# A linear-attention and Swish layer on one core: the order of work under the first output phase rearranged

## Chip, cores and metric

The kernel runs on one core of one Trainium2 chip. The metric is the device time of an execution in microseconds (us). TensorE's granted clock was 1.00 in the profile before. Times are medians of 3 to 12 runs. A ratio is the mean time of one kernel's fast runs over that of the other's fast runs of the same rounds, so it isn't quite the ratio of the medians quoted beside it.

## The reference

Linear attention with phi(x) = elu(x) + 1, then a two-layer product with Swish between, over 8 batches of 576 tokens, 8 heads of 64, and 2048 hidden features.

```python
def _attn_ref(q, k, v):                     # [8, 8, 576, 64] each
    phi = lambda x: np.where(x > 0, x, np.exp(x) - 1.0) + 1.0
    q_p, k_p = phi(q), phi(k)
    kv  = np.einsum('bhsd,bhse->bhde', k_p, v)
    num = np.einsum('bhsd,bhde->bhse', q_p, kv)
    den = np.einsum('bhsd,bhd->bhs', q_p, np.sum(k_p, axis=2))[..., None] + 1e-06
    return num / den
# x = attention output as [4608, 512]
h = x @ w_in                                # [512, 2048]
g = h * (1.0 / (1.0 + np.exp(-beta * h)))
out = g @ w_out                             # [2048, 512]
```

## The kernel before

The program is one hand-ordered stream per engine. For each batch b there are two phases on TensorE: Hb (x @ w_in, followed by Silu on ScalarE) and Yb (g @ w_out). The attention of batch b+1 is slipped in between the matmuls of both by a plan: a table from a step to functions that run after that step. Silu is called with scale beta, so w_out is divided by beta once, in four quarters (`w_out_scale`), as soon as each has landed. w_out lands in fp32 in buffers that later hold other things.

Two PSUM (matmul output memory) pairs of banks serve attention (`attps`, tag "att"), four single banks the large products. The last four groups of H0 borrow both pairs.

```python
    def w_out_scale(i, dve=True):
        for c in range(4):
            ...                                   # dst, src, by = rbeta[:, ff]
            if dve:
                nc.vector.tensor_scalar(dst, src, by, None, ALU.mult)
            else:
                nc.scalar.activation(dst, src, ACTF.Copy, scale=by)

    def h_last(b, x, between):
        hps = []
        for i in range(2):
            hp = att_banks()
            for ii in range(2):
                h_mm(b, x, hp[:, ii], 12 + 2 * i + ii, 0, 4)
                hps.append(hp[:, ii])
        for f in between:
            f()
        for i in range(4):
            silu(b, 12 + i, hps[i])

    def y_phase_wide(b, plan):                    # four tiles side by side, ff outermost
        yp = [mm_bank([P, DM]) for _ in range(4)]
        for ff in range(12):
            for t in range(4):
                y_mm(b, yp[t], t, ff)
            run(plan, ff)
        for t in range(4):
            for ff in range(12, FC):
                y_mm(b, yp[t], t, ff)
            y_out(b, t, yp[t], on_act=True)
            run(plan, 12 + t)

    # loads on GpSimd's queue, in this order: ... w_out 0, w_out 1, k 1, q 1, then
    load_w_out(2)
    load_v(1)
    load_w_out(3)
    # H0's plan (cut)
            17: [F(w_out_scale, 0)],
            19: [F(begin, 1), F(relu, 1, 1), F(relu, 1, 0)],
    # then
    clear_tail(2)
    load_next(2)
    h_last(0, xT[0], [F(exp_, 1, 1), F(exp_, 1, 0), F(w_out_scale, 2, dve=False)])
    w_out_scale(1)
    y_phase_wide(0, {
        4: [F(phi, 1, 1), F(v_copy, 1), F(phi, 1, 0), F(load_next, 3)],
        8: [F(kv_mm, 1), F(kv_evac, 1)],
        9: [F(q_trans, 1, 0, 1, wide=True), F(q_trans, 1, 2, 3, wide=True),
            F(w_out_scale, 3)],
        ...
    })
```

An index such as `relu, 1, 1` means batch 1, operand 1 (k); operand 0 is q. "KV" below is the product of phi(k) and v (`kv_mm`); its copy out of PSUM is `kv_evac`.

## Time and profile before

| | before |
|---|---|
| device time, median of 3 | 299.17 us (298.81 to 299.87) |
| profiled span | 297.2 us |
| TensorE busy | 284.8 us, 96% |
| ScalarE, VectorE busy | 177.2 and 125.0 us |
| Y0 on TensorE, from its first matmul to H1's first | 34.12 to 54.91 us |
| the same work by the spacing of matmuls | 17.63 us |

In the rows of a timeline the columns are: start, length from the first start to the last end, engine, source line, operation, output and inputs, and a count; in brackets stands the idle time of the engine before the row and what ended it. A row without brackets followed the one before it with hardly any idle time (the shortest that was printed is 0.16 us). L500 is a matmul of Y, L448 of H, L339 KV, L375 the transposes of phi(q), L394 the num products, L428 the transposes of x. On the other engines, L228 is an exp, L440 a Silu, L211 and L213 the scaling of w_out, L236 a relu, L241 phi, L350 the copy of KV, L410 the last step of a normalisation. A few matmul records are missing from each trace, so that a count of 3 or 15 can stand for 4 or 16. The rows themselves are in the prediction.

### The profile page before, as it was taken

What the parts mean: (1) busy time and instruction counts of PE and PEld (TensorE: products, weight loads), DVE (VectorE), ACT (ScalarE), POOL (GpSimd) and SP (SyncE); (2) the same over time, 40 slices, a digit from 0 to 9 for tenths busy, and PEclk for the clock granted to TensorE, in tenths of its full rate; (3) what the DMA queues carried; (4) which work ended last, traced back from release to release, by engine and by line L of the source; (5) the groups of instructions that cost most, each with busy time, mean ns of one, the idle gap of its engine ahead of it and who ended that gap; (6) DMA issues with size and microseconds to landing.
All of it is one profiled execution on the core that took longest, in us unless ns stands there. A gap on an engine that the chain in (4) does not pass through costs nothing.

```text
span 297.2 us, 4721 instructions
## 1 busy us (share of the span) xinstructions
PE 284.8 (96%) x1876; PEld 144.6 (49%) x1897; DVE 125.0 (42%) x263; ACT 177.2 (60%) x235; POOL 52.1 (18%) x72
## 2 busy tenths in 40 slices
PE   8789978999999999999999999999999999999994
PEld 3466435744556454445444544454445444444443
DVE  5774298504574154715471547154715400110012
ACT  2788795879988790779076907690660068008500
POOL 8925465723004100140011000000000000000000
PEclk9999999999999999999999999999999999999999
DMA  7999999999928954599457255024502400020032
GB/s 110 192 207 342 258 270 191 240 208 187 149 89 170 185 95 117 124 154 160 115 124 82 71 117 124 1 73 115 120 5 72 117 36 0 35 84 25 0 72 72
DMA packets 69206, 36.43 MB, mean 123 GB/s; under 512 B 37808, under 2 KB 63680, under 8 KB 69184
## 3 DMA queue, kind: packets, MB, share of 16 engines
q0 software_dynamic: 38400, 20.45, 47.4%
q1 hardware_dynamic: 30624, 15.55, 20.0%
q8 instruction: 15, 0.25, 0.3%
q10 hardware_dynamic: 160, 0.13, 0.2%
q14 instruction: 7, 0.06, 0.1%
HBM read 36.71 MB, written 9.44 MB: 155 GB/s over the span
## 4 chain that ended last, share of the span: by engine, by line
PE 71%; DMA 17%; ACT 6%; POOL 3%; issue 2%; DVE 0%; POOLq 0%; ACTq 0%
PE mm L448 33%; PE mm L500 32%; DMA xqk<-in_q_dram 5%; DMA xqk<-in_k_dram 4%; DMA vraw<-in_v_dram 4%; DMA w_in<-in_moe_w_in_dram 4%; PE att L394 2%; ACT e L228 2%; PE att L339 2%; POOL xqk L132 1%; PE mm L532 1%; ACT g L440 1%; ACT L228 1%; ACT w_out L213 1%; POOL vraw L132 1%
## 5 line engine op out<-in xcount | busy, mean ns | idle before, releaser
L440 ACT ACTIVATE g<-mm,beta_c 128x512 bf16<-128x512 f32 (+2 forms) x156 | 97.4, 632 | 88.4 <-PE mm L448 87.9
L500 PE MATMUL mm<-w_out,g 128*128 128x512 bf16 x541 | 127.5, 379 | 2.5 <-DVE w_out L211 1.3
L448 PE MATMUL mm<-xT,w_in 128*128 128x512 bf16 (+2 forms) x560 | 107.8, 349 | 1.0 <-DVE xT L365 0.5
L448 PEld LDWEIGHTS <-w_in 128*128 128x128 bf16 x656 | 62.2, 98 | 61.9 <-issue 0.9
L500 PEld LDWEIGHTS <-g 128*128 128x128 bf16 x560 | 52.8, 98 | 58.5 <-issue 1.6
L510 DVE COPY y_sb<-mm 128x512 f32<-128x512 f32 x27 | 18.7, 691 | 70.4 <-PE mm L500 68.2
L228 ACT ACTIVATE e<-xqk 128x2560 bf16<-128x2560 bf16 x14 | 31.9, 2329 | 0.1
L410 DVE TENSOR_TENSOR xs<-att,rden 128x512 bf16<-128x512 f32 (+1 forms) x40 | 27.6, 689 | 1.6 <-DVE rden L409 0.2
L241 DVE TENSOR_TENSOR qk_p<-r,e 128x2560 bf16<-128x2560 bf16 x14 | 20.9, 1490 | 14.6 <-ACT e L228 13.9
L350 DVE CAST kv_bd<-att 64x130 bf16<-64x130 f32 x28 | 8.2, 292 | 35.0 <-PE att L339 34.7
L72 POOL DMA_DIRECT2D vraw<-in_v_dram x7 | 6.2, 881 | 78.3 <-DVE vaug L365 70.9
L408 DVE TENSOR_SCALAR den<-att 128x8 f32<-128x8 f32 (+1 forms) x40 | 6.5, 161 | 27.1 <-PE att L394 27.0
L394 PEld LDWEIGHTS <-q_pT 128*128 128x128 bf16 (+1 forms) x160 | 11.7, 100 | 10.9 <-issue 2.7
L394 PE MATMUL att<-kv_bd,q_pT 128*128 128x130 bf16 (+1 forms) x160 | 15.8, 221 | 1.1 <-ACT q_pT L367 0.4
L236 DVE TENSOR_SCALAR r<-xqk 128x2560 bf16<-128x2560 bf16 x14 | 11.9, 858 | 7.2 <-DMA xqk<-in_k_dram 4.9
L448 PE MATMUL mm<-xT_tail,w_in 128*128 128x512 bf16 x63 | 13.9, 379 | 0.1
L567 PE MATMUL mm<-g 128*128 128x512 bf16 x35 | 10.0, 440 | 1.2 <-DVE g L144 1.2
L228 ACT ACT_TABLE_LOAD x7 | 9.0, 1283 | 1.6 <-DMA xqk<-in_k_dram 1.5
L409 DVE RECIPROCAL rden<-den 128x8 f32<-128x8 f32 (+1 forms) x40 | 8.1, 202 | 1.4
L72 POOL DMA_DIRECT2D xqk<-in_k_dram x7 | 6.2, 891 | 12.8 <-ACT e L228 6.5
L76 POOL DMA_DIRECT2D xqk<-in_k_dram x7 | 7.6, 1082 | 2.7 <-DMA w_in<-in_moe_w_in_dram 2.7
L440 ACT ACT_TABLE_LOAD x6 | 7.7, 1283 | 0.1
(73 smaller groups left out, 140.5 us busy)
## 6 DMA issues: line engine op xcount, KB each, us to landing
out_dram<-y_sb SPq DMA_DIRECT2D x28, 256.0 KB, 2.3
xqk<-in_k_dram POOLq DMA_DIRECT2D x7, 512.0 KB, 10.7
xqk<-in_q_dram POOLq DMA_DIRECT2D x7, 512.0 KB, 12.0
vraw<-in_v_dram POOLq DMA_DIRECT2D x7, 512.0 KB, 11.5
w_in<-in_moe_w_in_dram POOLq DMA_DIRECT2D x4, 512.0 KB, 11.5
g<-in_moe_w_out_dram POOLq DMA_DIRECT2D x4, 512.0 KB, 11.0
out_dram<-y_sb SPq DMA_DIRECT2D x14, 128.0 KB, 5.1
xqk<-in_moe_w_out_dram POOLq DMA_DIRECT2D x2, 512.0 KB, 14.8
```

The lines of the kernel that those rows point to most:

```text
L72: eng.dma_start(out=dst[:, :, 0:NJ, :].rearrange("p h j d -> p h (j d)"), in_=src[b, :, 0:MAIN, :].rearrange("h (p j) d -> p h (j d)", j=NJ),)
L228: nc.scalar.activation(st[b, "e", a][:, h0:h1], xqk[b % NX][:, a, h0:h1], ACTF.Exp)
L236: nc.vector.tensor_scalar(st[b, "r", a][:, h0:h1], xqk[b % NX][:, a, h0:h1], 0.0, 1.0, ALU.max, ALU.add)
L241: nc.vector.tensor_tensor(st[b, "p"][:, a].rearrange("p j (h d) -> p h j d", h=H)[:, h0:h1], st[b, "r", a][:, h0:h1], st[b, "e", a][:, h0: ...
L350: nc.vector.tensor_copy(kv_bd[b % 2][i][gs, :, g, :], st[b, "kvp"][gs, 2 * i : 2 * i + 2, :])
L394: nc.tensor.matmul(nps[:n, p // 2, c0 : c0 + 2 * (D + 1)], st[b, "qT"][:, t, p, :n], kv_bd[b % 2][p // 2][:, p % 2], start=True, stop=True ...
L410: nc.vector.tensor_mul(xs[:n], nv[:, :, :, 0:D], rden[:n, :, :, None].to_broadcast([n, 2, 4, D]))
L440: nc.scalar.activation(g_sb[b % 2][:, ff, c0:c1], hp[:, c0:c1], ACTF.Silu, scale=beta_c[:, ff : ff + 1],)
L448: nc.tensor.matmul(hp[:, c0:c1], w_in_sb[ff // 4][:, kc, (ff % 4) * P : (ff % 4 + 1) * P], x[:, t0:t1, kc, :] if b < B else x[:, kc, c0:c1 ...
L500: nc.tensor.matmul(yp, g_sb[b % 2][:, ff, t * P : (t + 1) * P], w_out_sb[ff // 4][:, ff % 4, :], start=(ff == 0), stop=(ff == FC - 1),)
L510: nc.vector.tensor_copy(y_sb, yp)
L567: nc.tensor.matmul(st["warm"], g_sb[0][:, FC - 1, 0:P], g_sb[0][:, FC - 1, :], start=True, stop=True, skip_group_check=True,)
```

## The change

Its intent is to take three waits of TensorE out of Y0: that for the second quarter of w_out, that of KV for the Silus, and that of the first num product.

```diff
     h_phase(0, ...,
-            3: [F(x_trans, 0, 1), F(num_mm, 0, 2), F(num_norm, 0, 2)],
+            3: [F(x_trans, 0, 1, dve=True), F(num_mm, 0, 2), F(num_norm, 0, 2),
+                lambda: q_out0(3, st["qb2"], 256, False)],     # was on VectorE, earlier
...
-            17: [F(w_out_scale, 0)],
-            19: [F(begin, 1), F(relu, 1, 1), F(relu, 1, 0)],
+            17: [F(w_out_scale, 0), F(w_out_scale, 1)],
     clear_tail(2)
     load_next(2)
-    h_last(0, xT[0], [F(exp_, 1, 1), F(exp_, 1, 0), F(w_out_scale, 2, dve=False)])
-    w_out_scale(1)
+    h_last(0, xT[0], [])
+    begin(1)
+    exp_(1, 1)
+    exp_(1, 0)
+    silu_table()
+    relu(1, 1)
+    relu(1, 0)
+    w_out_scale(2)
+    phi(1, 1)
+    v_copy(1)
+    phi(1, 0)
     y_phase_wide(0, {
-        4: [F(phi, 1, 1), F(v_copy, 1), F(phi, 1, 0), F(load_next, 3)],
-        8: [F(kv_mm, 1), F(kv_evac, 1)],
-        9: [F(q_trans, 1, 0, 1, wide=True), F(q_trans, 1, 2, 3, wide=True),
-            F(w_out_scale, 3)],
-        10: [F(q_trans, 1, 4, wide=True), F(num_mm, 1, 0), F(num_norm, 1, 0)],
-        11: [F(num_mm, 1, 1), F(num_norm, 1, 1)],
-        12: [F(num_mm, 1, 2), F(num_norm, 1, 2), F(x_trans, 1, 0, wide=True)],
-        13: [F(num_mm, 1, 3), F(num_norm, 1, 3), F(x_trans, 1, 1, wide=True)],
-        14: [F(num_mm, 1, 4), F(num_norm, 1, 4), F(x_trans, 1, 2, wide=True)],
+        4: [F(load_next, 3)],
+        9: [F(kv_mm, 1), F(kv_evac, 1), F(w_out_scale, 3)],
+        10: [F(q_trans, 1, 0, 1, wide=True), F(q_trans, 1, 2, 3, wide=True)],
+        11: [F(num_mm, 1, 0), F(num_norm, 1, 0)],
+        12: [F(num_mm, 1, 1), F(num_norm, 1, 1), F(x_trans, 1, 0, wide=True)],
+        13: [F(num_mm, 1, 2), F(num_norm, 1, 2), F(x_trans, 1, 1, wide=True)],
+        14: [F(num_mm, 1, 3), F(num_norm, 1, 3), F(q_trans, 1, 4, wide=True)],
     })
     h_phase(1, ..., {
+            0: [F(x_trans, 1, 2), F(num_mm, 1, 4), F(num_norm, 1, 4)],
             1: [F(x_trans, 1, 3)],
```

On VectorE `clear_tail(2)`, a memset of 0.48 us, stood behind the relus and now stands ahead of them, since the relus moved.

More of the change, by code (lines that the diff above doesn't have):

```diff
@@ L641, in q_second @@
         q_out0(2, qb2, 0, False)
-        q_out0(3, qb2, 256, True)
+        st["qb2"] = qb2
     h_phase(
```

## The prediction

> **What bounds the kernel now.** I read the page first, then the table of stretches, then the timelines of TensorE, ScalarE and VectorE from 30 to 56 us, then the waits of that stretch. The page settles how much can be had at all:
>
> ```profile
> PE 284.8 (96%) x1876; PEld 144.6 (49%) x1897; DVE 125.0 (42%) x263; ACT 177.2 (60%) x235; POOL 52.1 (18%) x72
> PE   8789978999999999999999999999999999999994
> PEclk9999999999999999999999999999999999999999
> ```
>
> TensorE is busy for 284.8 of 297.2 us at full clock. So only 12.4 us of the span are without a matmul in flight, and the change touches two stretches of it. The table of stretches places these 12.4 us (its columns: stretch, its length, then busy time of each engine):
>
> ```profile
> 10.00:19.80 9.80, 6.60 (x118) 4.83 (x119) 7.12 (x18) 6.75 (x15) 5.23 (x7) 1.00 1.25 202
> 19.80:34.10 14.30, 14.30 (x115) 9.32 (x113) 6.18 (x17) 11.48 (x24) 6.78 (x9) 1.00 1.30 273
> 34.10:54.90 20.80, 18.20 (x154) 9.78 (x156) 15.45 (x32) 16.64 (x21) 11.39 (x15) 1.00 1.44 242
> 54.90:69.30 14.40, 14.40 (x89) 8.15 (x88) 2.33 (x4) 12.53 (x21) 5.74 (x5) 1.00 1.48 225
> ```
>
> Y0 of batch 0 is 34.10 to 54.90 and idles 2.60 us; H0 after the start-up (19.80 to 34.10) and H1 (54.90 to 69.30) idle not at all. From there on the kernel is matmuls back to back, so whatever Y0 gives up should reach the end, and nothing else can be gained. The timeline of TensorE in Y0 (columns: start, length, what, idle before and its releaser):
>
> ```profile
> 34.12 3.62 PE L500 MATMUL mm<-w_out,g 128*128 128x512 bf16 x15
> 39.04 4.48 PE L500 MATMUL mm<-w_out,g 128*128 128x512 bf16 x20 [1.30 <-DVE w_out L211]
> 43.98 0.82 PE L339 MATMUL att<-vaug,qk_p 128*64 128x65 bf16 x40 [0.47 <-ACT g L440]
> 44.97 0.81 PE L500 MATMUL mm<-w_out,g 128*128 128x512 bf16 x3 [0.16 <-issue]
> 48.25 0.39 PE L394 MATMUL att<-kv_bd,q_pT 128*128 128x130 bf16 x4 [0.44 <-ACT q_pT L367]
> ```
>
> The 0.379 us of a matmul includes a drain that overlaps the next; successive starts are 0.2155 us apart: the x20 row is 19 x 0.2155 + 0.379 = 4.47. By spacing, Y0 needs 64 matmuls x 0.2155 = 13.79, the 40 small ones of KV 0.76, q transposes 0.90 + 0.22, five num products 4 x 0.235 + 0.355, three x transposes 0.66: 17.63 us of the 20.79 between 34.12 and 54.91. The loss is thus 3.16 us: 1.47 before the second group of w_out (16 matmuls end issue at 37.57; the row prints 15, one record is missing), 0.63 before KV, 0.50 before the first num product, 0.28 before an x transpose, and about 0.26 in crumbs. The 0.16 after KV is no loss: its group of four has three records.
>
> **What ends the waits.** ScalarE and VectorE in the same stretch:
>
> ```profile
> 33.05 1.28 ACT L228 ACT_TABLE_LOAD   x1 [1.49 <-DMA xqk<-in_k_dram]
> 34.34 4.56 ACT L228 ACTIVATE e<-xqk 128x2560 bf16<-128x2560 bf16 x2
> 38.81 2.54 ACT L213 ACTIVATE w_out<-g,rbeta 128x512 bf16<-128x512 f32 x4
> 41.37 1.28 ACT L440 ACT_TABLE_LOAD   x1
> 42.67 2.42 ACT L440 ACTIVATE g<-att,beta_c 128x512 bf16<-128x512 f32 x4
> 46.26 2.22 ACT L367 ACTIVATE q_pT<-att 128x1024 bf16<-128x1024 bf16 x3 [1.17 <-PE att L375]
> ```
>
> ```profile
> 36.32 1.27 DVE L236 TENSOR_SCALAR r<-xqk 128x2560 bf16<-128x2560 bf16 x1 [2.29 <-DMA xqk<-in_q_dram]
> 38.27 1.99 DVE L211 TENSOR_SCALAR w_out<-xT,rbeta 128x512 bf16<-128x512 f32 x4
> 41.95 0.98 DVE L365 COPY vaug<-vraw 128x2560 bf16<-128x2560 bf16 x1 [0.29 <-DMA vraw<-in_v_dram]
> 42.86 1.47 DVE L241 TENSOR_TENSOR qk_p<-r,e 128x2560 bf16<-128x2560 bf16 x1
> 44.84 1.21 DVE L350 CAST kv_bd<-att 64x130 bf16<-64x130 f32 x4 [0.52 <-PE att L339]
> 46.08 1.67 DVE L211 TENSOR_SCALAR w_out<-g,rbeta 128x512 bf16<-128x512 f32 x4
> ```
>
> The scaling of w_out's second quarter stands on VectorE behind two relus that wait for k and q of batch 1 (33.0 and 36.3 us); its own data landed near 28.9 and 30.2 us, where the load queue's waits for it end. The last four Silus stand on ScalarE behind exps, a scaling and a table load, and KV waits for the PSUM pair they free (43.9).
>
> **What the Trainium skill says.** "ScalarE: Activation LUTs", section What ACT_TABLE_LOAD costs, gives about 1283 ns for a load and some 1380 ns more for a drain. The trace agrees with the first (1.28) and not with the second as idle time: the exp follows its load by 0.01 us. I count 1.28 for a switch. "SBUF — State Buffer", section Who interferes with whom, says that a VectorE tensor_scalar in a two-port mode and GpSimd block each other. So scaling beside descriptor writing may stretch; the trace has 1.99 us for four at 38.27 (while loads are issued) against 1.67 at 46.08, and I take 2.0. "Perfetto Trace Analysis", section Identifying the Most-Contended Engine, warns that matmul busy share is no measure of headroom; hence the sum by spacing above.
>
> **The change part by part.**
> 1. Second quarter scaled ahead of the relus: ready at about 31.2 (landing 30.2 + two of 0.5). TensorE needs it at 37.57. The 1.47 us go entirely.
> 2. Third quarter moves from ScalarE (2.54) to VectorE, behind the q relu: 37.6 + 2.0 = 39.6, or 39.9 if its second half lands only at 38.9, where the queue issues the load that waits for it. TensorE gets to it at 34.1 + 32 x 0.2155 = 41.0. No wait, with 1.1 to 1.4 to spare.
> 3. Silus first: PSUM is filled at 34.3, so the last Silu ends near 34.9 rather than 45.1. Then table 1.28 to 36.2, exps 2.3 each to 38.5 and 40.8, table and dummy 1.5 to 42.3. The count of switches here stays at two. KV no longer waits for Silu.
> 4. What takes its place: phi of k at 39.7 to 41.2, then the v copy at 41.95, since v lands then whatever the order, to 42.93; phi of q to 44.35. KV moves to after ff 9, due at 34.1 + 40 x 0.2155 = 42.7, and waits for v until about 43.0: 0.3 instead of 0.63. It ends at 43.75; ff 10 takes TensorE to 44.6.
> 5. The copy of KV out of PSUM now follows phi of q on VectorE: 44.4 to 45.6. Of the two PSUM pairs for attention it holds one; the first q transposes take the other at 44.6 to 45.1, and the second ones wait for the copy: about 0.5 us, a new wait (0.06 now). They end at 46.1, ff 11 at 47.0, the first num product follows without the old 0.50.
> 6. Fourth quarter scaled 45.6 to 47.3; ff 12 starts at 47.2 and takes chunks in order. VectorE does a normalisation in 0.17 + 0.20 + 0.69 = 1.1 us with its gaps, starting at 47.3, while TensorE has 0.86 of y plus 0.23 and 0.22 per round, so it is paced by VectorE and the two pairs: about 0.2 before the first x transpose, 0.25 before the last num product in Y0, 0.1 elsewhere.
> 7. The third x transpose (0.22) and the fifth num product (0.355) move into H1. Same work, later: no gain in itself. ScalarE gets one copy of 0.6 more at H1's start, where it needs 0.42 per 256-column Silu against TensorE's 0.43. I allow 0.1 for a late bank.
> 8. In H0 one copy goes from VectorE to ScalarE and one the other way. The x transpose's copy takes 0.43 on VectorE against 0.60, so the group that waits until 19.36 may start 0.18 earlier; the normalisation behind it is 0.2 later and takes most of that back at 20.3. I count 0.05.
>
> Sum: old loss 3.16, new 0.3 + 0.5 + 0.2 + 0.25 + 0.1 + 0.1 = 1.45. Gain 3.16 - 1.45 + 0.05 = 1.76. The same walked as a clock puts Y0's end at 52.5 rather than 54.9, 0.575 of that moved into H1, and the last x transpose of batch 1 some 1.9 us earlier. I take 1.85: 299.17 - 1.85 = 297.3.
>
> **The rivals.**
> A, VectorE becomes Y0's pace: it now carries 2.0 more (15.45 + 2.0 of some 18.5 us). For it: phi, v copy, KV copy and scaling form one unbroken queue from 41.95 to 47.3. If it slips 0.5 at its head, every step of 5 and 6 slips as well, the num products too: gain about 1.0, 298.2 us. Against: its head is a landing that the change doesn't move.
> B, the gain is eaten by DMA: loads later than now, because VectorE's scaling falls on the issue of batch 2's loads. The page has 7 to 9 tenths of DMA share here. A late v by 1 us costs 1 us: 298.3. Against: as many scalings fell there before.
> C, no new waits: KV's copy gets in early, all 3.16 and 0.2 of H0 are gained, 295.8. Against it is the v landing, which binds in both kernels.
> D, H1 gives back: ScalarE late with Silus and four banks full. It would cost up to 0.5; later stretches would be unaffected.
>
> **Range and chances.** The runs of before spread by 1.1 us, and A and B reach 298.3; C alone reaches below 296. Eight in ten: 296.3 to 298.4. 2% is 6.0 us, nearly twice the whole loss of Y0, so faster by 2% would need a cause that the profile doesn't show: 0.01. Slower by 2% would need a new stall of 6 us: 0.01. Within 2%: 0.98.
>
> **What would show it.** Step 1: no wait of TensorE on w_out near 37.6. Step 3: Silu from PSUM pairs ends near 35. Step 4: KV begins near 43.0, released by the v copy. Step 5: a wait near 45.1 that KV's copy on VectorE ends. Step 6: small waits on xs. Step 7: H1 starts near 52.5. If KV begins well before 42.9, or if later stretches change by more than 0.3 us, my picture is wrong.

## The result and the profile after

| | before | after |
|---|---|---|
| device time, median | 299.11 us (4 runs) | 296.98 us (4 runs, 296.6 to 297.14) |
| ratio | | 0.9923, 95% interval 0.9902 to 0.9944 |
| profiled span | 297.2 us | 295.3 us |
| Y0 on TensorE | 34.12 to 54.91: 20.79 us | 34.27 to 52.28: 18.01 us |
| last x transpose of batch 1, in H1, starts | 56.98 | 55.03 |

By the rule of 2% the two are the same; the difference, 2.1 us of the medians, is clear of the noise and inside the predicted range. Not all of it lies in the stretch that the profile covers. Over all executions with a listed span (23 of the kernel before from the rounds below, 10 of the changed one) the mean device time fell from 299.00 to 296.93 us, and the mean span from 296.87 to 295.16. So about 1.7 us were gained inside the span and 0.36 outside it. The part of the device time outside the span is 2.06 to 2.23 us in every execution of the kernel before and 1.73 to 1.82 in the changed one. No trace shows what it consists of, so these 0.36 us stay unexplained. The table of stretches of the changed kernel (columns: stretch, its length, busy time of TensorE, its weight loads, VectorE, ScalarE and GpSimd with instruction counts, granted clock, DMA share, GB/s):

```profile
33.90:52.30 18.40, 17.75 (x149) 9.46 (x151) 13.69 (x29) 13.79 (x16) 10.93 (x13) 1.00 1.43 250
```

Y0 now has 0.65 us without a matmul in flight instead of 2.60. The same table gives Y1 18.22 busy us of 18.90 in both kernels: the gain inside the span is Y0's but for 0.12 us in H0, and it isn't given back later. It can be read from KV: the last x transpose of batch 1 comes 1.95 us earlier, because KV starts 0.98 earlier (43.98 to 43.00) and the stretch from KV to that transpose is 0.97 shorter (13.00 to 12.03). Of the 0.97, 0.86 are the four matmuls of one more step that now run ahead of KV (4 x 0.2155). The timeline of TensorE of the changed kernel in Y0:

```profile
34.27 8.80 PE L500 MATMUL mm<-w_out,g 128*128 128x512 bf16 x39
43.00 0.82 PE L339 MATMUL att<-vaug,qk_p 128*64 128x65 bf16 x40
...
45.49 0.62 PE L375 MATMUL att<-identity,qk_p 128*128 128x128 bf16 x8 [0.26 <-DVE kv_bd L350]
...
48.43 0.40 PE L428 MATMUL att<-identity,xs 128*128 128x128 bf16 x4
...
52.28 0.60 PE L448 MATMUL mm<-xT,w_in 128*128 128x256 bf16 x4
```

The first row is what the change wanted: 40 matmuls in one run, no wait at w_out. KV is due at 34.27 + 40 x 0.2155 = 42.89 and starts at 43.00. The first eight transposes start at 44.62, 0.056 apart, so the second eight were due at 45.07 and wait 0.42 until 45.49, for VectorE's copy of KV: the new wait of the prediction's step 5. VectorE and ScalarE of the changed kernel:

```profile
41.90 1.01 DVE L365 COPY vaug<-vraw 128x2560 bf16<-128x2560 bf16 x1 [0.70 <-DMA vraw<-in_v_dram]
42.84 1.47 DVE L241 TENSOR_TENSOR qk_p<-r,e 128x2560 bf16<-128x2560 bf16 x1
44.23 1.20 DVE L350 CAST kv_bd<-att 64x130 bf16<-64x130 f32 x4
45.47 1.71 DVE L211 TENSOR_SCALAR w_out<-g,rbeta 128x512 bf16<-128x512 f32 x4
...
47.68 0.69 DVE L410 TENSOR_TENSOR xs<-att,rden 128x512 bf16<-128x512 f32 x1
```

```profile
34.47 1.26 ACT L440 ACTIVATE g<-att,beta_c 128x512 bf16<-128x512 f32 x2 [0.46 <-PE att L448]
35.75 1.28 ACT L228 ACT_TABLE_LOAD   x1
37.05 4.56 ACT L228 ACTIVATE e<-xqk 128x2560 bf16<-128x2560 bf16 x2
```

VectorE is idle for 0.70 us until v lands at 41.90, and then works with hardly a break to 48.37, when the first normalised tile is done; TensorE transposes it at 48.43. So the path through Y0 in the changed kernel is a landing, then VectorE's queue up to the copy of KV. After that two paths are level: VectorE ends the scaling at 47.18 (45.47 + 1.71), TensorE ends the first num product at 47.20 (46.81 + 0.39), and the normalisation needs both.

### The profile page after: what moved, and what is told of

Its sections match the earlier page's. It is cut to its first block, busy times and chain, and to the rows that moved or that the text cites. A ratio compares the mean times of both kernels' runs of the same rounds, so it can differ in the third digit from the quotient of the medians.

```text
span 295.3 us, 4721 instructions
## 1 busy us (share of the span) xinstructions
PE 284.6 (96%) x1876; PEld 144.7 (49%) x1897; DVE 126.1 (43%) x267; ACT 175.0 (59%) x232; POOL 52.8 (18%) x72
## 4 chain that ended last, share of the span: by engine, by line
PE 72%; DMA 14%; POOL 5%; ACT 4%; issue 3%; DVE 1%; POOLq 0%; ACTq 0%; DVEq 0%
PE mm L500 33%; PE mm L448 33%; DMA vraw<-in_v_dram 9%; DMA xT<-in_moe_w_out_dram 5%; PE att L394 3%; ACT e L228 2%; POOL xqk L132 1%; PE att L339 1%; PE mm L532 1%; POOL w_in L160 1%; ACT L228 1%; POOL vraw L132 1%; POOL vraw L72 1%; ACT g L440 1%; DVE qk_p L241 0%
## 5 line engine op out<-in xcount | busy, mean ns | idle before, releaser
L241 DVE TENSOR_TENSOR qk_p<-r,e 128x2560 bf16<-128x2560 bf16 x14 | 20.8, 1489 | 13.1 <-ACT e L228 12.4
L228 ACT ACT_TABLE_LOAD x7 | 9.0, 1283 | 0.1
L72 POOL DMA_DIRECT2D xqk<-in_q_dram x7 | 6.5, 922 | 6.6 <-DMA xqk<-in_k_dram 2.5
```

Source lines behind the costliest of these rows:

```text
L72: eng.dma_start(out=dst[:, :, 0:NJ, :].rearrange("p h j d -> p h (j d)"), in_=src[b, :, 0:MAIN, :].rearrange("h (p j) d -> p h (j d)", j=NJ),)
L228: nc.scalar.activation(st[b, "e", a][:, h0:h1], xqk[b % NX][:, a, h0:h1], ACTF.Exp)
L241: nc.vector.tensor_tensor(st[b, "p"][:, a].rearrange("p j (h d) -> p h j d", h=H)[:, h0:h1], st[b, "r", a][:, h0:h1], st[b, "e", a][:, h0: ...
```

## The experiments

Twelve kernels ran in three rounds of four. The kernel before had medians of 298.92, 299.03 and 299.09 us in these rounds. Five of the experiments' executions had a mean clock of 0.991 to 0.994; each was the slowest of its kernel by 0.4 to 2.2 us. They stay in the medians and ratios below, and the text says where that matters. The first round (the second quarter alone and behind the relus, the third quarter, the plan) had no run of the changed kernel; its kernels are held against the 296.95 us of the second round. In all experiments 1.72 to 2.01 us lie outside the span, as in the changed kernel, but for three: the second quarter alone and the two kernels with all copies of KV on ScalarE have 2.07 to 2.23, like the kernel before. Where this matters, the span is given too. My theory at this point: the waits of Y0 stand behind one another on one path, anchored by landings (k before, v after), so that they don't add. The rival is the bookkeeping of my own prediction: each wait is worth its length.

**The changed kernel again**, as the yardstick of the second round.

> The changed kernel once more, on the chip of the three that follow, as their yardstick. Theory (the slack before KV is nearly used up, so a late start of TensorE now reaches the end, while the kernel before hid it behind its wait for the Silus): median near 297.0 with a wider spread than the kernel before, now and then 1 to 2 us longer when the start-up before H0 ran long. Rival: as narrow as before, within 0.6 us.

Measured: 296.95 us (296.67 to 297.2, 6 runs), ratio 0.993 (0.9917 to 0.9944). The gain repeats. The spread was as narrow as the rival said, so the first theory about spread failed here. It isn't refuted in general: of the 12 executions of two kernels below that are as fast (the second quarter behind the relus, and H0's exchange undone), one each took 299.7, at a clock of 0.994 and 0.991. Its TensorE:

```profile
33.80 8.80 PE L500 MATMUL mm<-w_out,g 128*128 128x512 bf16 x40
42.96 0.82 PE L339 MATMUL att<-vaug,qk_p 128*64 128x65 bf16 x40 [0.36 <-DVE vaug L365]
```

In this execution TensorE entered Y0 0.47 us earlier than in the first profile of the same kernel (33.80 against 34.27), and reached KV and H1 at the same times (42.96 and 43.00, 52.27 and 52.28). The row names the v copy as what KV waits for.

**The second quarter ahead of the relus, alone**, in the kernel before.

```diff
-            17: [F(w_out_scale, 0)],
+            17: [F(w_out_scale, 0), F(w_out_scale, 1)],
...
-    w_out_scale(1)                       # behind h_last
```

> The kernel before with one thing changed: the second quarter of w_out is scaled ahead of the relus. Theory (waits of one chain stand behind one another): TensorE no longer waits near 37.6, runs to the end of ff 8 at about 41.9, and then waits some 2.1 us before KV until the Silus free the PSUM pair at about 44.0, as before. Gain 0.0 to 0.2 us: 299.0. Rival (each wait is worth its length): the 1.47 us are gained, 297.6.

Measured: 299.03 us against 298.92, ratio 1.0001 (0.9988 to 1.0014): no gain at all. TensorE of this run:

```profile
35.04 7.93 PE L500 MATMUL mm<-w_out,g 128*128 128x512 bf16 x36
43.99 0.82 PE L339 MATMUL att<-vaug,qk_p 128*64 128x65 bf16 x40 [1.02 <-ACT g L440]
```

The wait at w_out is gone, 36 matmuls run through, and KV starts at 43.99, where it started at 43.98 before. TensorE even entered Y0 0.92 us later here than in the profile of before, and that too left no trace after KV. The longest wait of the old Y0 was worth nothing by itself: whatever TensorE gained there it waited for the Silus.

**The second quarter behind the relus again**, in the changed kernel; the tail clearing stays ahead of them.

```diff
-            17: [F(w_out_scale, 0), F(w_out_scale, 1)],
+            17: [F(w_out_scale, 0)],
...
     relu(1, 0)
+    w_out_scale(1)
     w_out_scale(2)
```

> The changed kernel with the second quarter scaled behind the relus again (the other parts stay). Theory (VectorE's queue up to the v copy sets KV): the first chunk is ready at about 37.8, so TensorE waits less than 0.4 us at w_out; but the third quarter and phi of k slip by 2 us, phi of k ends at about 42.8 and the v copy at 43.8, so KV waits 0.8 us more than in the changed kernel and the normalisations slip alike: 0.8 to 1.2 us slower than the changed kernel, about 297.9. Rival (the old wait returns as it was): 1.5 us at w_out, about 298.4, with nothing more before KV.

Measured: 297.02 us (6 runs; 297.01 without a low-clock one of 299.67), ratio 0.9954 (0.9928 to 0.998). Both expectations failed: it isn't to be told from the changed kernel (median span 295.25 and 295.2). TensorE, then VectorE:

```profile
34.28 8.80 PE L500 MATMUL mm<-w_out,g 128*128 128x512 bf16 x40
```

```profile
35.99 0.83 DVE L236 TENSOR_SCALAR r<-xqk 128x2560 bf16<-128x2560 bf16 x1 [2.15 <-DMA xqk<-in_q_dram]
36.73 2.07 DVE L211 TENSOR_SCALAR w_out<-xT,rbeta 128x512 bf16<-128x512 f32 x4
38.72 2.06 DVE L211 TENSOR_SCALAR w_out<-g,rbeta 128x512 bf16<-128x512 f32 x4
```

KV again starts at 43.00. The scaling starts at 36.73 rather than 38.27, so its first chunk is in time for 37.73. The three idle stretches that VectorE has in the changed kernel (0.21 and 0.41 for w_out, 0.70 for v, 1.3 us together) take up most of the 2.07 us, and this profile's q landed 0.3 us earlier. I had left these gaps out of the expectation.

**All of VectorE's old order**: relus, then the tail clearing, then the second quarter.

```diff
-            17: [F(w_out_scale, 0), F(w_out_scale, 1)],
+            17: [F(w_out_scale, 0)],
-    clear_tail(2)
     load_next(2)
...
     relu(1, 0)
+    clear_tail(2)
+    w_out_scale(1)
     w_out_scale(2)
```

> The changed kernel with VectorE's old order in full ahead of the third quarter: relus, then the 0.48 us clearing of the next tail, then the second quarter. (With the clearing ahead of the relus, putting the second quarter behind them cost nothing.) Theory (VectorE has some 1.3 us of slack before v lands, and the first chunk was in time by less than 0.5): the first chunk is ready near 38.3, TensorE waits 0.4 to 0.8 us at w_out, phi of k ends near 43 and the v copy near 43.9, so KV comes 0.7 to 1.2 us later: 0.7 to 1.3 us slower than the changed kernel, about 297.9. Rival (VectorE's order ahead of v doesn't matter): the same within 0.2.

Measured: 298.62 us (297.96 to 299.32), ratio 0.9984 (0.9967 to 1.0). The theory's direction holds; the size is 1.7 us above 296.95, and 1.3 was the most expected. The profiled run was the slowest of the six, and its loads landed late (k at 33.6):

```profile
39.23 5.36 PE L500 MATMUL mm<-w_out,g 128*128 128x512 bf16 x24 [0.70 <-DVE w_out L211]
44.91 0.82 PE L339 MATMUL att<-vaug,qk_p 128*64 128x65 bf16 x40 [0.32 <-DVE vaug L365]
```

The old wait for w_out is back, and KV starts at 44.91. This trace alone doesn't single out the memset: q landed 0.94 us later than in the profile of the run before, and the four scalings took 2.70 instead of 2.07. The times do, since the two kernels differ only in the memset's place and even the fastest execution here, 297.96, is 1.3 above the other's fastest, 296.63. Why it costs 1.7 and not 1.3 at most stays open. The median span, 296.8, is that of the kernel before, so all that the change gains inside the span is gone. Behind the relus the second quarter is late only with the memset in front of it; with the other parts of the change in place, moving the memset ahead is enough, which is why undoing the quarter alone had cost nothing. The reverse, the quarter ahead and the memset behind, was tried only in the kernel before.

**The third quarter on ScalarE again**, behind the exps, in the changed kernel.

```diff
     exp_(1, 0)
+    w_out_scale(2, dve=False)
     silu_table()
     relu(1, 1)
     relu(1, 0)
-    w_out_scale(2)
```

> The changed kernel with the third quarter of w_out scaled on ScalarE behind the exps again, so with Silus first but without the move to VectorE. Theory: the exps end at about 41.6, the first chunk at 42.3, TensorE waits 1.1 us before ff 8, KV comes at about 44.1 and its copy out ends 0.7 us later; part of it replaces the old waits at KV and at the q transposes. 0.6 to 1.1 us slower than the changed kernel, about 297.8. Rival (VectorE is the pace of this stretch, so taking 2 us of work off it pays): same or faster, 296.9 or less.

Measured: 297.85 us (6 runs; 297.76 without one of 299.91 at a clock of 0.994), ratio 0.9976 (0.9952 to 1.0001): 0.8 to 0.9 us slower than the changed kernel, as the theory said, though the executions at a full clock scatter from 297.17 to 299.06. The low-clock execution is the profiled one and entered Y0 late, at 36.19; the wait is still plain in it:

```profile
44.20 1.89 PE L500 MATMUL mm<-w_out,g 128*128 128x512 bf16 x8 [0.94 <-ACT w_out L213]
```

From Y0's first matmul to H1's it takes 18.75 us (36.19 to 54.94) against 18.01.

**The order of Silus and exps undone**, in the changed kernel: exps first again, the third quarter still on VectorE.

```diff
-    h_last(0, xT[0], [])
     begin(1)
-    exp_(1, 1)
-    exp_(1, 0)
-    silu_table()
+    h_last(0, xT[0], [F(exp_, 1, 1), F(exp_, 1, 0)])
```

> The changed kernel with ScalarE's old order: exps of batch 1 ahead of the last four Silus of H0; the third quarter's scaling stays on VectorE. Theory (the gain came from taking 2.54 us of scaling off ScalarE and from the later plan, not from the order of Silus and exps): exps from 34.3 to 38.9, table load to 40.2, Silus to 42.7, still before KV's start at 43.0, which the landing of v sets; the same as the changed kernel within 0.2 us, about 297.0. Rival (Silus first is the heart of the change): KV waits for the Silus as before, 0.6 to 1 us slower, about 297.8.

Measured: 296.74 us (296.5 to 297.37), ratio 0.9929 (0.9915 to 0.9944): as fast as the changed kernel. ScalarE of this run:

```profile
33.78 4.56 ACT L228 ACTIVATE e<-xqk 128x2560 bf16<-128x2560 bf16 x2
...
39.66 2.42 ACT L440 ACTIVATE g<-att,beta_c 128x512 bf16<-128x512 f32 x4
```

The Silus end at 42.08, before KV's start at 42.78 in this run. (v landed early here, at 41.39; with a landing at 41.90 KV would start near 43.0 and the Silus would still be done.) In the kernel before they ended at 45.09 because 2.54 us of scaling stood ahead of them, and the first two, for which KV waits, ended near 43.9. The first words of the change, Silus first, are the part that isn't needed; taking the scaling away from in front of them is.

**The plan under Y0 undone**, in the changed kernel: the old plan from step 8 on, and nothing of batch 1 added to H1.

```diff
-        9: [F(kv_mm, 1), F(kv_evac, 1), F(w_out_scale, 3)],
+        8: [F(kv_mm, 1), F(kv_evac, 1)],
...      # and so on to step 14, as before
```

> The changed kernel with the old plan under Y0 (KV after ff 8, all five tiles of batch 1 finished up to three x transposes within Y0). Theory: v lands at 41.9 whatever the order, so KV due at 42.0 waits about 0.9 us instead of 0.1, and the num products and normalisations bunch up again; 0.7 to 1.2 us slower than the changed kernel, about 297.9. Rival (the plan doesn't matter, only the order on ScalarE and VectorE does): the same as the changed kernel, 296.9.

Measured: 297.91 us (297.09 to 298.2), ratio 0.9961 (0.9949 to 0.9974): 0.9 us slower, as the theory said. The profile fell on the fastest execution, at 297.09, and shows why that one was fast: v landed at 41.20 instead of 41.90.

```profile
42.10 0.82 PE L339 MATMUL att<-vaug,qk_p 128*64 128x65 bf16 x40
```

So in that execution KV lost only 0.1 us. The 0.9 us that I expected KV to lose with a normal landing is therefore not seen in a trace; the median agrees with it. The trace does show what the plan is worth behind KV: from KV's start to the last x transpose of batch 1 it takes 12.99 us (42.10 to 55.09) against 12.03 in the changed kernel. As 0.86 of this is the step that stands behind KV again, an estimate from these figures is that KV's place makes nearly all of the plan's effect, and its other moves 0.1.

**v loaded later**, in the changed kernel: the direct test of the anchor.

```diff
     load_w_out(2)
-    load_v(1)
     load_w_out(3)
+    load_v(1)
```

> The changed kernel with batch 1's v loaded behind the last quarter of w_out instead of ahead of it. Theory (the landing of v sets KV, and with it the end of Y0): v is issued 3.8 us later, at about 32.7, lands at about 44.2, KV starts at about 45.3 instead of 43.0, 1.8 to 2.5 us slower than the changed kernel, about 299.1. Rival (VectorE's queue or TensorE itself sets KV, and v has time to spare): under 0.5 us slower.

Measured: 299.46 us (6 runs; 299.27 without one of 300.31 at 0.993), ratio 1.0019 (1.0004 to 1.0034): 2.5 us slower than the changed kernel. VectorE, then TensorE:

```profile
44.24 0.83 DVE L365 COPY vaug<-vraw 128x2560 bf16<-128x2560 bf16 x1 [2.89 <-DMA vraw<-in_v_dram]
```

```profile
45.12 0.82 PE L339 MATMUL att<-vaug,qk_p 128*64 128x65 bf16 x40 [1.91 <-DVE vaug L365]
```

v lands 2.34 us later, KV starts 2.12 us later, and the whole gain of the change is gone. This shows that v's landing is the anchor of the changed kernel, with no slack to speak of. TensorE's own arrival is nearly level with it: where TensorE entered Y0 late, at 34.62 (the split below) and 34.92 (H0's exchange undone), KV started at 43.35 and 43.64, at the end of the 40 matmuls, and not when v was copied (42.95 and 43.09).

**The copy of KV split** between ScalarE (two) and VectorE (two), in the changed kernel, and **the copy all on ScalarE**.

```diff
     def kv_evac(b):
...
-                nc.vector.tensor_copy(dst, src)
+                copy(dst, src, b != 1 or i == 1)      # split; for all on ScalarE: b != 1
```

> The changed kernel with two of the four copies of batch 1's KV out of PSUM on ScalarE, idle there between 43.1 and 45.3, and two on VectorE. Theory (the second q transposes wait 0.4 us because this copy queues on VectorE behind phi of q): the copy ends near 44.9 instead of 45.4, the wait of TensorE at the transposes goes and scaling and normalisations start 0.6 us earlier: 0.4 to 0.6 us faster than the changed kernel, about 296.5. Rival (the wait is handed on to the next PSUM pair, freed by ScalarE's q copies): under 0.2 us.

> As the split copy, with all four copies on ScalarE. Theory: four times 0.29 from 43.9 end at 45.0, before the first q copy at 45.2, so the transposes don't wait either; and VectorE starts the fourth scaling at 44.3 instead of 45.5: 0.4 to 0.7 us faster than the changed kernel. Rival (ScalarE becomes late with its q copies): the gain of the transposes comes back before the first num product, under 0.2 us.

Measured: 296.77 us (ratio 0.9925, 0.9912 to 0.9938) and 296.9 us (0.9931, 0.9917 to 0.9944), against 296.95 (0.993) in the same round. Neither gain is resolved by the times; both are below 0.2 us, as the rivals said. But with all copies on ScalarE the mean span is 294.80 us against the changed kernel's 295.16, near the 0.4 us of the theory; the part outside the span is longer by about as much (2.07 to 2.21 instead of 1.73 to 1.82). VectorE with the split, then TensorE with all on ScalarE:

```profile
44.81 0.60 DVE L366 CAST kv_bd<-att 64x130 bf16<-64x130 f32 x2 [0.47 <-ACT kv_bd L368]
```

```profile
44.78 1.06 PE L376 MATMUL att<-identity,qk_p 128*128 128x128 bf16 x16
...
48.15 0.40 PE L429 MATMUL att<-identity,xs 128*128 128x128 bf16 x4
```

The split doesn't run side by side: as the program is built, VectorE's half waits for ScalarE's, and its queue is no earlier than before. With all copies on ScalarE the 16 transposes run in one piece, the wait is gone, and from KV's start to H1's start it takes 8.86 us instead of 9.28; the first x transpose comes 0.28 earlier. So the wait that I predicted at the transposes was real and can be removed. Inside the span it is worth some 0.3 to 0.4 us. There VectorE is done with the scaling at 46.47 and then waits 0.49 us for the num product, so TensorE, not VectorE's queue, sets the first x transpose. The part outside the span takes the gain back in the times, for a reason that no trace shows.

**The exchange of copies in H0 undone.**

```diff
-            3: [F(x_trans, 0, 1, dve=True), F(num_mm, 0, 2), F(num_norm, 0, 2),
-                lambda: q_out0(3, st["qb2"], 256, False)],
+            3: [F(x_trans, 0, 1), F(num_mm, 0, 2), F(num_norm, 0, 2)],
...
-        st["qb2"] = qb2
+        q_out0(3, qb2, 256, True)
```

> The changed kernel without the exchange of copies in H0. Theory: H0 itself is some 0.12 us longer, but TensorE's wait for v before KV takes it up wherever there is one; 0.0 to 0.12 us slower than the changed kernel, not to be told from it by the times. Rival (the exchange matters for the whole of H0): over 0.3 us slower.

Measured: 297.0 us (6 runs; 296.95 without one of 299.66 at a clock of 0.991), ratio 0.9946 (0.9919 to 0.9974): not to be told from the changed kernel. Its trace does show H0: from its first matmul to Y0's it takes 17.62 us (17.30 to 34.92), as in the kernel before (16.50 to 34.12), against 17.50 in the changed one (16.77 to 34.27).

**A version meant to be faster than both**: all copies of KV on ScalarE, and the v copy in two halves, so that KV can start on the first.

```diff
     phi(1, 1)
-    v_copy(1)
+    v_copy(1, 0, H // 2)
+    v_copy(1, H // 2, H)
     phi(1, 0)
```

> The changed kernel with all four copies of KV on ScalarE, and the v copy in two halves, so that KV's first half starts on the first. Theory: the all-on-ScalarE copy took 0.4 us out of the stretch from KV to H1 by the trace, the halves let KV start up to 0.4 us earlier when TensorE is early enough: 0.3 to 0.7 us faster than the changed kernel, about 296.4. Rival (TensorE's own start is the limit by now): under 0.3 us.

Measured: 297.24 us (6 runs; 297.1 without one of 298.87 at 0.994), ratio 0.9945 (0.9924 to 0.9967): a miss; it isn't faster than the changed kernel. Its profile is of the low-clock execution, which entered Y0 at 36.13. The stretch of that profile from 15 to 20 us (the table's last three columns are granted clock, DMA share and GB/s), then VectorE in Y0:

```profile
15.00:20.00 5.00, 4.22 (x46) 2.64 (x45) 3.82 (x11) 4.05 (x8) 1.54 (x3) 0.76 1.25 208
```

```profile
41.28 1.49 DVE L241 TENSOR_TENSOR qk_p<-r,e 128x2560 bf16<-128x2560 bf16 x1 [1.37 <-ACT e L228]
```

The granted clock was 0.76 there, where the changed kernel's profile has 1.00 in the same stretch; H0 ends late, the Silus end late, and the exps behind them hold up phi of k by 1.37 us. From KV's start to H1's start it takes 8.86 us (44.86 to 53.72), just as with the copies on ScalarE. The executions at a full clock were as slow as 297.61, and no trace of one of them was taken. Their spans tell more: their mean is 294.96 us, 0.2 below the changed kernel's, and 2.07 to 2.20 us of the device time lie outside it, some 0.35 more than in the changed kernel. So the small gain of the trace is there, and what lies outside the span takes it back; why stays open.

## Why the prediction was right, and where its steps were not

The total was right: 1.85 us were predicted, and the medians differ by 2.13. The closeness is in part luck: about 1.7 us were gained inside the span, which is what the steps describe, and 0.36 outside it, which no step foresaw. Counted in the two profiles as in the prediction, H0's exchange gives 0.12. Y0's loss falls from 3.16 to 18.01 - (17.63 - 0.575) = 0.96 us, and H1's start loses 0.10 more than before: 2.2 us in all. The last x transpose of batch 1, measured from Y0's start, says the same: 22.86 us before, 20.76 after. The start-up before H0 was 0.27 us longer in the profile after, so on the clock the transpose is 1.95 earlier.

- **Step 1** (the 1.47 us at w_out "go entirely"): as a statement about the wait it held, as a term of the sum it failed. Alone the step gained nothing, and undone it cost nothing. The wait lay ahead of another one, for the Silus, on a path that didn't begin with it; and in the changed kernel moving the memset out of the way was enough by itself. The loss of the whole phase, before minus after, was a sound sum; to read one wait in it as what its part is worth was not, since the waits don't add.
- **Step 2** held: the scaling was done at 39.81, 1.4 us before its use, and putting it back costs 0.8 to 0.9 us. The prediction booked this move as costless; by the single undoings it is one of the two parts that the gain needs.
- **Step 3** held for KV, which no longer waits for Silus. Its time was off, since the Silus of a pair wait until both of its banks are written: the last ended at 35.73 instead of 34.9 and the exps at 41.61 instead of 40.8, which cost nothing. The order itself, which the step took for the cause, isn't: with exps first the kernel is as fast, as long as ScalarE doesn't scale.
- **Step 4** held to 0.1 us: v landed at 41.90, KV began at 43.00, and moving v by 2.34 us moved KV by 2.12. With the old plan the kernel is 0.9 us slower: KV's later step, which makes nearly all of the plan's effect, is the other part that the gain needs.
- **Step 5** held: 0.42 us where 0.5 was predicted, with the releaser named. It is worth some 0.3 to 0.4 us inside the span, and that doesn't reach the times.
- **Step 6** was too high: the first x transpose waited 0.28 (48.15 to 48.43; 0.2 was predicted), but the last num product of Y0 0.02 instead of 0.25. This and KV's wait (0.11 instead of 0.3, step 4) make the 0.4 us by which the new loss was smaller than predicted.
- **Step 7** held: H1 began at 52.28 (52.5 was predicted), and its start lost 0.10 us more than before.
- **Step 8**: H0 gained 0.12 in the profile where 0.05 was predicted, and with the exchange undone the trace has the old length again; the times can't show it.

Of the rivals, A described the changed kernel best: from v's landing to the copy of KV, VectorE's queue is the pace. It didn't lower the gain, because the head of that queue didn't slip. Its premise of 2.0 us more work was a misreading: the second quarter (1.99 us) leaves Y0 as the third comes in, and VectorE's busy time went from 15.45 us in the old Y0 to 13.69 in the new one. B's fear was right about the anchor, and v's landing was simply where it had been; delaying it took the whole gain away. C and D didn't come. Two smaller readings were off too: the table of stretches places 5.8 of the 12.4 us without a matmul (3.20 and 2.60), not all of them, and in Y0 the page's row for DMA has nine tenths throughout, not 7 to 9.

The single undoings cost 0 (quarter), 0.9 (third quarter), 0.9 (plan), 0 (order on ScalarE) and 0 (H0) of the 2.1 us, but the quarter together with the memset costs 1.7. These numbers can't be added into a total either, and no experiment changed two of the larger parts at a time.

## What to carry to other kernels

Before a wait is put into a sum, follow the path behind it to the next point that something else fixes, here a landing or a queue that starts with one; a wait ahead of such a point is worth only what the point itself moves. Test the anchor by shifting it by a known amount: one swapped load order told more here than five undone parts. And look at what a reordering does to the small instructions that aren't in the diff's headline; a memset of 0.48 us decided whether one of the named parts mattered.

## What the Trainium skill lacked or had wrong

- "ScalarE: Activation LUTs", What ACT_TABLE_LOAD costs: the load's 1283 ns agree (1.28 in every row), but the 1380 ns of drain beside it don't show. In the changed kernel a Silu ends at 35.73, the load runs from 35.75, and the exp starts at 37.05: 1.32 us from the end of one function to the start of the next, not 2.66.
- "SBUF — State Buffer", Who interferes with whom, says that one of the two engines fully blocks while both want the shared port, and gives no size for a queue of short instructions. Here four scalings of 128x512 took 1.66 us in the quietest case and up to 2.70 (both in the kernel with VectorE's old order, the second while loads of batch 2 were issued), a relu of 128x2560 0.83 to 1.27, and the first issue of batch 2's k on GpSimd 0.89 in the kernel before and 1.53 in the changed one. That the port is the cause is the page's reading; no run here tested it.
- "TensorE: Matmul & The Clock Gate", HAM oscillation — how this bites in real kernels, gives as its rule that a kernel should have no gaps of TensorE above about 3.4 us. Five of 74 executions of the changed kernel and the experiments had a mean clock of 0.991 to 0.994, and two of these were profiled. In both the granted clock fell to 0.50 during the start-up (14 to 17 us in the last version, 13 to 15 with the third quarter on ScalarE), and the gap just before it was only 1.55 and 2.02 us. Gaps of 1.75 and 1.78 us in two other profiles (VectorE's old order, the second quarter alone) left the clock at 1.00, so the length of the gap doesn't decide it here; what does stays open.
- No page that I know gives the scatter of landings between executions of one program under a queue of loads: v of batch 1, issued at the same place in the order, landed between 41.2 and 42.0 us where VectorE was seen to wait for it. With a kernel anchored to a landing this goes straight into its time.
- No page that I know says why the part of the device time outside the profiled span should differ between orders of the same work: here it was 1.72 to 2.01 us in nine kernels and 2.06 to 2.23 in four.
